# A convolution and mixer kernel: one idle product less ahead of the band, masks moved, and the low-rank sums of batch 0 regrouped

## The chip, the cores and the metric

One core of one Trainium2 chip. The metric is device time in microseconds (us) of one execution; most executions of one kernel agree within 0.3%.

## The reference

```python
# x: (8, 4224, 192); weight: (8 heads, 7 taps); U: (4224, 32); V: (32, 4224)
w = softmax(weight)                          # per head
y = causal 7-tap convolution of x, per head  # 24 channels per head
h = y.transpose(0, 2, 1) @ U @ V             # low rank, over the sequence
u = y + h.transpose(0, 2, 1)
out = u + relu(u @ w_ch1) @ w_ch2            # 192 -> 768 -> 192
```

## The kernel before

The convolution runs on TensorE as a product with a banded matrix ("band"), built at the start in two halves of four heads each. Batch 0 is the prologue: nothing can overlap it. Its x comes in four pieces, each of some blocks of 64 rows; the low-rank sums `y^T U` of its 33 tiles follow as pieces finish. The parts that matter (cuts marked `...`):

```python
    zz = cst.tile([P, 512], F32, name="zz")
    nc.vector.memzero(zz[:])

    rq = cst.tile([P, 2], F32, name="rq")
    for r in range(4):
        for n, v in enumerate((32.0, -128.0)):
            nc.vector.memset(rq[QB * r : QB * r + QB, n : n + 1], v * r)
    wps = bank()

    def idle(n):
        for _ in range(n):
            nc.tensor.matmul(out=wps[:], lhsT=zz[:, 0:P], rhs=zz[:], start=True, stop=True)

    idle(5)
...                                  # VectorE makes ident, and the products pr of both halves
    Eq = cst.tile([P, 4, P], BF16, name="Eq")
    nc.vector.tensor_scalar(
        out=Eq[:], in0=efp[:], scalar1=rq[:, 1:2], scalar2=None, op0=ALU.is_equal
    )

    nc.vector.tensor_scalar(
        out=fp[:], in0=fp[:], scalar1=R - 1, scalar2=None, op0=ALU.bitwise_and
    )
    R4 = cst.tile([P, P], BF16, name="R4")
    nc.vector.tensor_scalar(
        out=R4[:], in0=fp[:], scalar1=0.0, scalar2=None, op0=ALU.is_equal
    )

    def band_half(hh):
        bp = bank()
        for d in range(KC):
            nc.tensor.matmul(
                out=bp[:, 0 : HQ * BW],
                lhsT=ident[:],
                rhs=prs[hh][:, d, :, :],
                start=(d == 0),
                stop=(d == KC - 1),
            )
        for r in range(4):
            o = QB * (r % 2)
            evac(
                "AD"[hh],
                bands[hh][QB * r : QB * r + QB, :, o : o + BW],
                bp[QB * r : QB * r + QB, 0 : HQ * BW].rearrange("p (h t) -> p h t", h=HQ),
            )
...
    band_half(0)
    idle(1)
    band_half(1)
...
    def tt_split(b, p):

        hi = sml.tile([P, D], BF16, name="tt_hi")
        lo = sml.tile([P, D], BF16, name="tt_lo")
        nc.scalar.activation(out=hi[:], in_=p[:, 0:D], func=ACT.Copy)
        nc.vector.tensor_tensor(out=lo[:], in0=p[:, 0:D], in1=hi[:], op=ALU.subtract)
        ttb[b] += [hi, lo]

    def tt_done(b, p):
        t = sml.tile([P, D], BF16, name="tt_sb", bufs=3)
        nc.vector.tensor_copy(out=t[:], in_=p[:, 0:D])
        ttb[b] = t
...
    for h in range(0, H, 2):
        conv(0, h, 2, [0, 1], "AA" if h == 0 else "AD", *KP[0][1:])
    work = [bank() for _ in range(4)]
    u_layout(work)
    x_tile(1)
    x_zero(1, nc.gpsimd)
    x_part(1, *XP[0])
...
    ps0 = bank()
    parts0 = [(0, 0, 2, bank(), "A"), (0, 2, 4, bank(), "D"), (1, 0, 4, bank(), "D")]
    yT_part(0, parts0)
    conv_piece(2, work[0:3])
    tt_mm(0, piece_tiles(0) + piece_tiles(1), work[3])
    tt_split(0, work[3])
    conv_piece(3, work[0:3])
    tt_late(ps0, late[0], 0, True, False)
    for part in ttb[0]:
        nc.tensor.matmul(out=ps0[:, 0:D], lhsT=R4[:], rhs=part[:], start=False, stop=False)
    tt_late(ps0, late[1], len(late[0]), False, True)
    more = [(2, 0, 2, bank(), "A"), (2, 2, 4, bank(), "A")]
    yT_part(0, more)
    tt_done(0, ps0)
    hT_part(0, parts0 + more)
```

`idle` products are fp32, and each shows as two passes in the traces (five products, x10); they only warm the array. `evac` copies a PSUM bank to SBUF on ScalarE ("A") or VectorE ("D"). There are eight banks, used in rotation. A sum "on column tiles" (`tt_mm`) uses 32 of the array's 128 columns, four tiles at a time; a "full-width" sum (`tt_late`) uses weights repeated four times. `tt_split` writes a sum as two bf16 parts, tt_hi on ScalarE and then tt_lo on VectorE; the two R4 products add the four column groups up.

## Time and profile before

| | kernel before |
|---|---|
| median of all 6 runs beside the changed kernel | 326.88 us (326.1 to 327.98) |
| span of the profiled execution | 325.0 us |
| first low-rank product on TensorE | 18.68 us |
| end of the last TensorE product | 320.96 us |
| landing of the last store | 323.88 us |

All positions are in us from the start of the span of the profiled execution. The prologue ends with the first low-rank product; the four last rows divide the span into a prologue (18.7), the steady stretch (302.3), the landing of the last stores (2.9) and a closing barrier (1.1). Copies of a kernel's result from a PSUM bank to SBUF are called evacuations below; a number like L365 is a line of the kernel.

### The profile page before, as it was taken

The numbers are of one execution on the slowest core, as the hardware profiler recorded it, in microseconds if no ns is written. First come the engines' busy times: TensorE is split into PE (matmuls) and PEld (weight loads), VectorE is DVE, ScalarE is ACT, GpSimd is POOL, SyncE is SP. The second block draws the span as 40 slices with busy tenths as digits, with TensorE's granted clock in tenths as the row PEclk, the third lists the DMA queues.
The fourth block names the chain that finished last, engine by engine and source line by source line (L and its number), as shares of the span: only waits on it lengthen the run. The fifth ranks groups of instructions, "written<-read, shape, count | busy, mean of one in ns | idle before, by whom it ended". The sixth has DMA issues, their size and how long they took to land.

```text
span 325.0 us, 9590 instructions
## 1 busy us (share of the span) xinstructions
PE 318.6 (98%) x3998; PEld 223.9 (69%) x3998; DVE 269.5 (83%) x552; ACT 170.1 (52%) x343; POOL 143.6 (44%) x112
## 2 busy tenths in 40 slices
PE   8999999999999999999999999999999999999995
PEld 3766676478677747867864784587796497497494
DVE  7759999987987986998798699879888898896863
ACT  1667624860775397088339609824904903903910
POOL 8684179729946694786859497000000000000000
PEclk9999999999999999999999999999999999999999
DMA  9999993998996899599699957139168069048044
GB/s 106 193 183 180 200 217 102 193 200 252 199 156 177 234 171 169 168 188 180 159 235 150 221 150 195 47 110 240 49 183 255 3 159 280 2 120 269 2 135 159
DMA packets 122907, 53.52 MB, mean 165 GB/s; under 512 B 87760, under 2 KB 122832, under 8 KB 122864
## 3 DMA queue, kind: packets, MB, share of 16 engines
q1 hardware_dynamic: 84528, 38.08, 46.3%
q0 software_dynamic: 38192, 14.73, 39.4%
q8 instruction: 31, 0.51, 0.6%
q14 instruction: 12, 0.10, 0.1%
q10 hardware_dynamic: 144, 0.10, 0.1%
HBM read 29.49 MB, written 25.95 MB: 171 GB/s over the span
## 4 chain that ended last, share of the span: by engine, by line
PE 94%; DVE 4%; ACT 1%; issue 0%
PE ps L579 42%; PE ps L550 39%; PE ps L335 3%; PE ps L453 3%; PE ps L155 2%; PE ps L398 2%; DVE rl_sb L566 1%; PE ps L365 1%; ACT rl_sb L564 1%; DVE y_sb L254 1%; DVE u_sb L475 1%; PE ps L520 0%; PE ps L505 0%; DVE band L254 0%; PE ps L678 0%; PE ps L424 0%
## 5 line engine op out<-in xcount | busy, mean ns | idle before, releaser
L564 ACT ACTIVATE rl_sb<-ps 128x512 bf16<-128x512 f32 x233 | 124.3, 604 | 108.0 <-PE ps L550 96.0
L579 PE MATMUL ps<-W_sb,rl_sb 128*128 128x192 bf16 x1584 | 141.9, 246 | 0.1
L579 PEld LDWEIGHTS <-rl_sb 128*128 128x128 bf16 x1584 | 128.0, 98 | 13.5 <-issue 13.0
L550 PE MATMUL ps<-uT,W_sb 64*128 64x512 bf16 x1188 | 131.7, 376 | 0.0
L566 DVE TENSOR_SCALAR rl_sb<-ps 128x512 bf16<-128x512 f32 x163 | 105.3, 687 | 15.7 <-PE ps L550 15.4
L550 PEld LDWEIGHTS <-W_sb 64*128 64x128 bf16 x1188 | 66.7, 94 | 60.6 <-issue 3.8
L588 DVE TENSOR_TENSOR out_sb<-ps,u_sb 128x384 f32<-128x384 f32 (+1 forms) x133 | 70.3, 549 | 25.7 <-PE ps L579 24.4
L301 POOL COPY xb_sb<-x_sb 32x3072 bf16<-32x3072 bf16 (+1 forms) x24 | 67.6, 2826 | 0.7
L475 DVE TENSOR_TENSOR u_sb<-y_sb,ps 128x192 bf16<-128x192 bf16 (+1 forms) x168 | 66.2, 459 | 0.0
L289 POOL COPY xb_sb<-x_sb 128x3072 bf16<-128x3072 bf16 x12 | 32.6, 2744 | 34.4 <-PE ps L335 25.7
L252 ACT ACTIVATE y_sb<-ps 128x408 bf16<-128x408 f32 (+4 forms) x89 | 37.8, 512 | 10.4 <-PE ps L335 7.8
L79 POOL DMA_DIRECT2D x_sb<-in_x_dram x32 | 27.1, 851 | 17.7 <-PE ps L550 10.8
L254 DVE CAST y_sb<-ps 128x408 bf16<-128x408 f32 (+4 forms) x37 | 19.7, 577 | 0.8 <-PE ps L365 0.7
L453 PE MATMUL ps<-tt_sb,V_sb 32*128 32x192 bf16 x264 | 12.4, 246 | 0.2 <-DVE y_sb L254 0.2
L335 PE MATMUL ps<-x_sb,band 64*32 64x384 bf16 x192 | 12.1, 333 | 0.0
L335 PE MATMUL ps<-xb_sb,band 64*32 64x384 bf16 x192 | 12.1, 332 | 0.0
L453 PEld LDWEIGHTS <-V_sb 32*128 32x128 bf16 x264 | 4.7, 92 | 7.5 <-issue 7.5
L155 PE MATMUL ps<-zz 128*128 128x512 f32 x12 | 8.2, 836 | 1.5 <-DVE zz L145 1.5
L412 ACT ACTIVATE tt_hi<-ps 128x192 bf16<-128x192 f32 x8 | 2.7, 332 | 11.2 <-PE ps L398 11.2
L365 PE MATMUL ps<-x_sb,band 64*64 64x240 bf16 (+3 forms) x192 | 8.0, 276 | 0.4 <-DVE band L254 0.4
L365 PEld LDWEIGHTS <-band 64*64 64x64 bf16 x192 | 6.0, 106 | 2.2 <-issue 1.2
L335 PEld LDWEIGHTS <-band 64*32 64x32 bf16 x384 | 4.5, 89 | 4.1 <-issue 3.0
(65 smaller groups left out, 72.9 us busy)
## 6 DMA issues: line engine op xcount, KB each, us to landing
out_dram<-out_sb SPq DMA_DIRECT2D x131, 192.0 KB, 2.7
x_sb<-in_x_dram POOLq DMA_DIRECT2D x14, 384.0 KB, 7.6
x_sb<-in_x_dram POOLq DMA_DIRECT2D x7, 432.0 KB, 7.3
x_sb<-in_x_dram POOLq DMA_DIRECT2D x7, 408.0 KB, 7.5
x_sb<-in_x_dram POOLq DMA_DIRECT2D x1, 504.0 KB, 7.5
uT<-u_sb SPq DMA_TRANSPOSE x31, 4.2
x_sb<-in_x_dram POOLq DMA_DIRECT2D x1, 480.0 KB, 5.7
W_sb<-in_moe_w_ch_dram POOLq DMA_DIRECT2D x2, 192.0 KB, 8.0
```

What stands on the lines that cost most here:

```text
L79: return nc.gpsimd.dma_start(out=xt[b][HB * r : HB * r + HB, s0:s1, :], in_=x[b, blk * HB : (blk + s1 - s0) * HB, :].rearrange("(j p) d -> ...
L252: nc.scalar.activation(out=out, in_=in_, func=ACT.Copy)
L289: nc.gpsimd.tensor_copy(out=xbt[b][:, s0:s1, :], in_=xt[b][:, s0 + 1 : s1 + 1, :])
L301: nc.gpsimd.tensor_copy(out=xbt[b][q, s0:s1, :], in_=xt[b][q, s0:s1, :])
L335: nc.tensor.matmul(out=pp[r][QB * cg : QB * cg + QB, 0 : nk[r] * GS], lhsT=w[hr], rhs=t[hr, st : st + 2 * nk[r] - 1 : 2, hs], start=True, ...
L453: nc.tensor.matmul(out=banks[pr][:, a * D : (a + 1) * D], lhsT=V_sb[32 * q : 32 * q + 32, (j // 8) * 2 + j % 2, :], rhs=ttb[b][32 * q : 32 ...
L475: nc.vector.tensor_tensor(out=u_group(g)[:, i : i + n, :, hf, :], in0=yt[b][:, run[0] : run[0] + n, :].rearrange("p n (c k) -> p n c k", c=3),
L550: last = nc.tensor.matmul(out=pps[m][hf][:], lhsT=W1_sb[HB * hf : HB * hf + HB, c, m * P : (m + 1) * P], rhs=uTt[g][HB * hf : HB * hf + HB ...
L564: nc.scalar.activation(out=rl[:, m, hf, :], in_=pp[hf][:], func=ACT.Relu)
L566: nc.vector.tensor_scalar_max(out=rl[:, m, hf, :], in0=pp[hf][:], scalar1=0.0)
L579: last = nc.tensor.matmul(out=cps[:, a * D : (a + 1) * D], lhsT=rlt[g][:, m, hf, (i + a) * P : (i + a + 1) * P], rhs=W2_sb[:, m, :], start ...
L588: nc.vector.tensor_tensor(out=o[:, 0:n, :].rearrange("p n (c k) -> p n c k", c=3), in0=cps[:, 0 : n * D].rearrange("p (n c k) -> p n c k", ...
```

## The change

Intent: take one idle product (and the start-up of a wide zero tile) out from ahead of the band, let VectorE evacuate the band's second half before it makes two masks that are needed later, and do 27 instead of 20 sums of batch 0 on column tiles, which are cheaper on TensorE than full-width ones.

```diff
@@ x pieces
-    KP = [(0, 0, 10), (1, 0, 10), (1, 10, NB1 // 2), (0, 10, NB0 // 2)]
+    KP = [{0: (0, 10), 1: (0, 10)}, {1: (10, NB1 // 2)}, {0: (10, NB0 // 2)}]
 ... (x_piece, piece_tiles, conv follow the new form; the same four loads in the same order)
@@ idle products
-    zz = cst.tile([P, 512], F32, name="zz")
+    zz = cst.tile([P, P], F32, name="zz")
-            nc.tensor.matmul(out=wps[:], lhsT=zz[:, 0:P], rhs=zz[:], start=True, stop=True)
-    idle(5)
+            nc.tensor.matmul(
+                out=wps[:].rearrange("p (n t) -> p n t", t=P),
+                lhsT=zz[:],
+                rhs=zz[:].unsqueeze(1).to_broadcast([P, 4, P]),
+                start=True,
+                stop=True,
+            )
+    idle(4)
@@ masks: these two move from ahead of band_half to behind u_layout(work)
-    nc.vector.tensor_scalar(
-        out=fp[:], in0=fp[:], scalar1=R - 1, scalar2=None, op0=ALU.bitwise_and
-    )
-    R4 = cst.tile([P, P], BF16, name="R4")
-    nc.vector.tensor_scalar(
-        out=R4[:], in0=fp[:], scalar1=0.0, scalar2=None, op0=ALU.is_equal
-    )
@@ sums of batch 0
-    late = [piece_tiles(k) for k in (2, 3)]
+    late = piece_tiles(2)
 ... (U4_sb and its copy shrink to the 6 tiles of late)
     work = [bank() for _ in range(4)]
+    tp = bank()
-    conv_piece(2, work[0:3])
-    tt_mm(0, piece_tiles(0) + piece_tiles(1), work[3])
-    tt_split(0, work[3])
-    conv_piece(3, work[0:3])
-    tt_late(ps0, late[0], 0, True, False)
-    for part in ttb[0]:
-        nc.tensor.matmul(out=ps0[:, 0:D], lhsT=R4[:], rhs=part[:], start=False, stop=False)
-    tt_late(ps0, late[1], len(late[0]), False, True)
+    conv_piece(1)
+    tt_mm(0, piece_tiles(0), tp, last=False)
+    conv_piece(2)
+    tt_mm(0, piece_tiles(1), tp, len(piece_tiles(0)))
+    tt_split(0, tp)
+    ps0 = work[3]
     more = [(2, 0, 2, bank(), "A"), (2, 2, 4, bank(), "A")]
-    yT_part(0, more)
+    yT_part(0, more[0:1])
+    tt_late(ps0)
+    for n, part in enumerate(ttb[0]):
+        nc.tensor.matmul(out=ps0[:, 0:D], lhsT=R4[:], rhs=part[:], start=False, stop=(n == 1))
+    yT_part(0, more[1:])
     tt_done(0, ps0)
```

More of the change, by code (lines that the diff above doesn't have):

```diff
@@ L84 @@
     XP = [(0, 1, 17), (0, 17, NB0 + 1), (1, 0, 18), (1, 18, NB1 + 1)]
-    KP = [(0, 0, 10), (1, 0, 10), (1, 10, NB1 // 2), (0, 10, NB0 // 2)]
+    KP = [{0: (0, 10), 1: (0, 10)}, {1: (10, NB1 // 2)}, {0: (10, NB0 // 2)}]
     def x_piece(k):
-        r, k0, k1 = KP[k]
-        x_part(0, r, (1 - r if k0 == 0 else 2 * k0 + 1), 2 * k1 + 1)
+        for r, (k0, k1) in KP[k].items():
+            x_part(0, r, (1 - r if k0 == 0 else 2 * k0 + 1), 2 * k1 + 1)
     def piece_tiles(k):
-        r, k0, k1 = KP[k]
-        return [NB0 // 2 * r + j for j in range(k0, k1)]
+        return [NB0 // 2 * r + j for r, ks in KP[k].items() for j in range(*ks)]
     x_tile(0)
-    for k in range(2):
-        x_piece(k)
+    x_piece(0)
     I32 = mybir.dt.int32
@@ L129 @@
     nc.gpsimd.dma_start(out=Ur[0:nlast, nfull, :], in_=U4[nfull * P :, :])
-    for k in range(2, len(KP)):
+    for k in range(1, len(KP)):
         x_piece(k)
@@ L349, in conv32, with conv @@
                 )
-    def conv(b, h0, nh, rs, engs, k0=0, k1=NT, pp=None):
+    def conv(b, h0, nh, rs, engs, ks=((0, NB0 // 2), (0, NB1 // 2)), pp=None):
         if yt[b] is None:
             yt[b] = ys.tile([P, NT, D], BF16, name="y_sb")
-        nk = {r: min(k1, (NB0, NB1)[r] // 2) - k0 for r in rs}
+        nk = {r: ks[r][1] - ks[r][0] for r in rs}
         if pp is None:
@@ L363, in conv @@
                     for c in range(2):
-                        st = 1 - halo + c + 2 * k0
+                        st = 1 - halo + c + 2 * ks[r][0]
                         last = nc.tensor.matmul(
@@ L381, in conv @@
         for n, r in enumerate(rs):
-            j0 = NB0 // 2 * r + k0
+            j0 = NB0 // 2 * r + ks[r][0]
             evac(
@@ L390, with tt_mm @@
     ttb = [[] for _ in range(B)]
-    def tt_mm(b, js, p=None):
+    def tt_mm(b, js, p=None, o=0, last=True):
         if p is None:
             p = bank()
-        for n, j in enumerate(js):
+        end = o + len(js)
+        for n, j in enumerate(js, o):
             c = n % 4
@@ L402, in tt_mm @@
                 start=(n < 4),
-                stop=(n + 4 >= len(js)),
+                stop=last and n + 4 >= end,
                 tile_position=(0, 32 * c),
@@ L669, with tt_late @@
         LOADS[b] = [(g, 0), (g, 3), (g + 1, 0), (g + 1, 3)]
-    late = [piece_tiles(k) for k in (2, 3)]
-    U4_sb = cst.tile([P, sum(len(js) for js in late), 4, R], BF16, name="U4_sb")
-    def tt_late(p, js, o, first, last):
-        for n, j in enumerate(js):
+    late = piece_tiles(2)
+    U4_sb = cst.tile([P, len(late), 4, R], BF16, name="U4_sb")
+    def tt_late(p):
+        for n, j in enumerate(late):
             nc.tensor.matmul(
                 out=p[:, 0:D],
-                lhsT=U4_sb[:, o + n, :, :].rearrange("p a r -> p (a r)"),
+                lhsT=U4_sb[:, n, :, :].rearrange("p a r -> p (a r)"),
                 rhs=yt[0][:, j, :],
-                start=first and n == 0,
-                stop=last and n + 1 == len(js),
-            )
-    def conv_piece(k, pps):
-        r, k0, k1 = KP[k]
-        for n, h in enumerate(range(0, H, 3)):
-            conv(0, h, min(3, H - h), [r], "AD"[n % 2], k0, k1, {r: pps[n]})
+                start=(n == 0),
+                stop=False,
+            )
     for h in range(0, H, 2):
-        conv(0, h, 2, [0, 1], "AA" if h == 0 else "AD", *KP[0][1:])
+        conv(0, h, 2, [0, 1], "AA" if h == 0 else "AD", KP[0])
     work = [bank() for _ in range(4)]
+    tp = bank()
     u_layout(work)
+    nc.vector.tensor_scalar(
+        out=fp[:], in0=fp[:], scalar1=R - 1, scalar2=None, op0=ALU.bitwise_and
+    )
+    R4 = cst.tile([P, P], BF16, name="R4")
+    nc.vector.tensor_scalar(
+        out=R4[:], in0=fp[:], scalar1=0.0, scalar2=None, op0=ALU.is_equal
+    )
     x_tile(1)
@@ L698 @@
     o = 0
-    for js in late:
+    for r, (k0, k1) in KP[2].items():
+        j = NB0 // 2 * r + k0
         nc.gpsimd.tensor_copy(
-            out=U4_sb[:, o : o + len(js), :, :],
+            out=U4_sb[:, o : o + k1 - k0, :, :],
             in_=U_sb[:]
-            .rearrange("p k j r -> p (k j) r")[:, js[0] : js[-1] + 1, :]
+            .rearrange("p k j r -> p (k j) r")[:, j : j + k1 - k0, :]
             .unsqueeze(2)
-            .to_broadcast([P, len(js), 4, R]),
+            .to_broadcast([P, k1 - k0, 4, R]),
         )
-        o += len(js)
+        o += k1 - k0
     NSL = (NT + 7) // 8 * 2
@@ L725, with conv_piece @@
     nc.gpsimd.dma_start(out=W2_sb[:], in_=moe_w_ch2[:].rearrange("(m p) d -> p m d", p=P))
-    ps0 = bank()
     parts0 = [(0, 0, 2, bank(), "A"), (0, 2, 4, bank(), "D"), (1, 0, 4, bank(), "D")]
     yT_part(0, parts0)
-    conv_piece(2, work[0:3])
-    tt_mm(0, piece_tiles(0) + piece_tiles(1), work[3])
-    tt_split(0, work[3])
-    conv_piece(3, work[0:3])
-    tt_late(ps0, late[0], 0, True, False)
-    for part in ttb[0]:
-        nc.tensor.matmul(out=ps0[:, 0:D], lhsT=R4[:], rhs=part[:], start=False, stop=False)
-    tt_late(ps0, late[1], len(late[0]), False, True)
-    more = [(2, 0, 2, bank(), "A"), (2, 2, 4, bank(), "A")]
-    yT_part(0, more)
+    def conv_piece(k):
+        for n, h in enumerate(range(0, H, 3)):
+            for r in KP[k]:
+                conv(0, h, min(3, H - h), [r], "AD"[n % 2], KP[k], {r: work[n]})
+    conv_piece(1)
[4 more added lines that the diff above has]
+    ps0 = work[3]
+    more = [(2, 0, 2, bank(), "A"), (2, 2, 4, bank(), "A")]
+    yT_part(0, more[0:1])
[3 more added lines that the diff above has]
+    yT_part(0, more[1:])
     tt_done(0, ps0)
```

## The prediction

> **What bounds the kernel now.** I read the busy table first, then the stretches of the span, then the chain of waits over the first 22 us, which is all that the change touches.
>
> ```profile
> PE 318.6 (98%) x3998; PEld 223.9 (69%) x3998; DVE 269.5 (83%) x552; ACT 170.1 (52%) x343; POOL 143.6 (44%) x112
> ```
>
> ```profile
> 21.00:38.00 17.00, 16.94 (x181) 10.41 (x180) 15.32 (x29) 11.54 (x24) 7.41 (x15) 1.00 1.49 181
> 38.00:160.00 122.00, 121.66 (x1647) 86.61 (x1644) 104.72 (x217) 70.91 (x148) 87.00 (x50) 1.00 1.07 188
> ```
>
> TensorE (first busy figure) has no holes from 21 us on: 16.94 of 17.00, 121.66 of 122.00. So the kernel is a prologue of 21 us and then 300 us of a full TensorE that the change leaves alone. Whatever the prologue gains, the end gains, once and no more: 1% of the span is 3.3 us, and the whole prologue is 21.
>
> The prologue's chain:
>
> ```profile
> 1.47 7.11 PE ps L155 x10
> 8.57 0.46 PE ps L232 x7
> 9.04 0.90 PE ps L155 x2
> 9.94 0.47 PE ps L232 x7
> ...
> 11.42 0.33 DVE band L254
> 11.75 0.04 issue
> 11.80 1.01 PE ps L365 x30
> 12.80 0.59 PE ps L260 x15
> 13.40 0.57 PE ps L505 x16
> 13.96 1.28 PE ps L365 x32
> 15.24 0.53 PE ps L398 x20
> 15.77 1.12 PE ps L365 x32
> 16.89 0.69 PE ps L678 x7
> 17.57 0.17 PE ps L736 x2
> 17.73 0.51 PE ps L678 x6
> 18.24 0.02 issue
> 18.27 0.37 DVE tt_sb L418
> ```
>
> L155 are the idle products (they warm the array and compute nothing), L232 builds the band, L365 is the convolution, L260 lays out U, L505 transposes y, L398 sums 20 tiles on column tiles, L678 sums 13 tiles with full-width weights. The reader should see that idle products stand directly ahead of both halves of the band, and that the convolution waits for VectorE's evacuation of half two.
>
> **What the Trainium skill says.** "TensorE: Matmul & The Clock Gate", Part 1, says that the array starts at half rate and reaches full rate after a busy window of some 3.4 us, and that this window is free-running. The trace agrees: idle passes start every 0.854 us until 6.69 us and every 0.429 us after. So the length of the idle stretch depends on where that switch falls in a run. "TensorEngine Tiling (Array Packing)", Tiling Modes, says that tiles work independently, up to four for 32 columns, and that a change of mode drains the array. The trace agrees: 20 column-tiled sums took 0.53 us of the chain (27 ns each), 13 full-width ones 0.69 + 0.51 = 1.20 us (92 ns each). The same page, PSUM Bottleneck, warns that tiling does not speed up evacuation, which is the warning that matters here. The skill has nothing that settles when the x pieces land; that I take from the trace.
>
> **The change part by part.**
>
> *Idle products.* Each is two passes. The zero tile shrinks from 512 to 128 columns; its memset took 0.48 us for 512 columns and a 256-column one 0.27, so about 0.17 us for 128: TensorE starts 0.31 earlier, at 1.16. One product less removes two late passes, 0.86 us at full rate. Eight passes from 1.16, six or seven of them slow, end near 7.38 instead of 8.41. VectorE's two products pr run 6.05 to 8.49, 1.26 each, so the first is ready at 7.3, just in time: half one of the band starts about 1.03 us earlier. The single idle product between the halves stays (0.90), so half two starts at 8.75 (its pr is ready at 8.49), also 1.03 earlier.
>
> *The masks.* fp and R4 (0.27 + 0.23 us on VectorE) move behind the U layout. Half two leaves TensorE at 9.4. VectorE was then free before as well (R4 ended at 9.34, the evacuation began at 10.44), so without the move the two would just have met; the move itself is worth 0 to 0.1 us. Evacuation ends at 10.72 instead of 11.75.
>
> *The x pieces.* They are issued in the same order and at the same times. The second one is the catch:
>
> ```profile
> 2.28 0.94 POOL L79 DMA_DIRECT2D x_sb<-in_x_dram  x1
> ...
> x_sb<-in_x_dram POOLq DMA_DIRECT2D x1, 504.0 KB, 7.5
> ```
>
> 2.28 + 7.5 = 9.8 us. The convolution started at 10.33, held by ScalarE's evacuation of half one (9.07 + 1.20 = 10.27). That now ends at 9.24, but the third product of the convolution reads the second piece, so it starts at about 9.85: of 1.03 us only 0.48 are left. The old stall for band half two goes, apart from under 0.1 us, so TensorE would end the convolution about 1.1 us earlier.
>
> *ScalarE then takes over.* It evacuates five of the eight convolution results, one every 0.47 us:
>
> ```profile
> 10.97 2.42 ACT L252 ACTIVATE y_sb<-ps 128x480 bf16<-128x480 f32 x5 [0.70 <-PE ps L365]
> 13.43 0.69 ACT L252 ACTIVATE U_sb<-ps 128x288 bf16<-128x288 f32 x2
> ```
>
> It began 0.64 us after the convolution did, so now at 10.49, and its queue is only 0.48 earlier. The buffers rotate through eight banks. The U layout's third product needs the bank freed by the third evacuation (10.49 + 1.49 = 11.98), the transposes' second part that of the fifth (12.91), and the next convolution piece the first U evacuation (about 13.37). TensorE arrives ahead of each and waits. So the second convolution piece starts at about 13.44 instead of 13.89: gain 0.45. Its x piece landed at 5.72 + 7.3 = 13.0, the next at 6.50 + 8.0 = 14.5, needed at 15.2; both hold.
>
> *The sums.* Order is now: piece (1.28), 20 sums (0.52), piece (1.12), 7 sums on column tiles, split, 6 full-width sums, two R4 products. Seven sums of 92 ns become seven of about 27: about 0.45 us less TensorE work. But the split now follows the last piece. Before, it lay under that piece (ScalarE at 15.82, VectorE at 16.18). Now ScalarE first finishes its last evacuation (17.34 before, so 16.90), then tt_hi (0.33) to 17.27, then VectorE tt_lo (0.36) to 17.66, and the second R4 product starts at 17.70. TensorE has only six sums to do meanwhile (16.95 to 17.45). The old path ran last evacuation 17.34, last sum started at 17.98: 0.64. The new one runs 16.90 to 17.70: 0.80. The regrouping thus loses some 0.16 us although it takes work off TensorE. tt_sb is ready at 18.34 instead of 18.63.
>
> Sum: +0.45 up to the second piece, -0.16 in the tail, 0.28 to 0.3 us gained at the first low-rank product. GpSimd's copy of U for the full-width sums shrinks from 13 tiles to 6 (0.93 us less), off the path: its loads are paced by landings.
>
> **The rivals.** *The whole of the idle time comes through:* 1.0 us, plus 0.4 from cheaper sums, so about 325.9. For it: L155 is on the chain, L678 too. Against: the landing at 9.8 and the evacuation queue. *The warm-up falls otherwise:* if the clock switches 1.5 us later, the old convolution starts near 11.1, the new one still near 9.9, and the gain is about 1 us; if it switches earlier, both wait for x and the tail's 0.16 us is lost: 327.4. *The tail costs more:* if the R4 products wait longer for the split, or TensorE's wait before the convolution dropped the clock, nothing is gained or 0.5 us lost: 327.5 to 328. The wait is about 0.6 us, short beside the 5 us that the start-up took, so I doubt the second.
>
> **Range and chances.** The runs of before spread from 326.25 to 327.57, mean 327.06. Less 0.28, with a little weight on the later switch, that is 326.8. The run-to-run spread of 0.7 either way and the rivals from 325.9 to 327.5 give 325.7 to 327.9. A gain over 2% needs 6.5 us, a third of the prologue; nothing here can give that. Faster 0.01, within 2% 0.98, slower 0.01.
>
> **What would show it right or wrong.** In the changed profile: idle products ending near 7.4; band half one at 7.4; the first convolution at 9.8 to 9.9, released by the landing and no longer by an evacuation; no stall of 0.36 for band half two; new short waits of TensorE on ScalarE in the U layout and the transposes; a wait on VectorE tt_lo before the last R4 product; tt_sb ending at about 18.3. I am wrong if the convolution starts before 9.7 (then x was not the limit), if the convolution pieces follow with no wait for ScalarE, if no wait on tt_lo appears, or if an idle gap over 0.2 us opens after 21 us, which would mean that the early gain is given back.

## The result, and the profile after

The changed kernel took 325.56 us in the median of 6 runs (325.4 to 325.79), the kernel before 326.88. The ratio is 0.9958 (95% interval 0.9935 to 0.998). Ratios here are the mean time of one kernel's fast runs over that of the other's of the same rounds, so not quite the ratio of the medians quoted. The gain is 1.4 us by the means (326.94 and 325.56), under 2% as foretold, but 325.56 lies below the stated range, which began at 325.7. The predicted gain of 0.28 us was five times too small.

The two profiled executions divide it:

| | before | after | difference |
|---|---|---|---|
| second convolution piece starts | 13.89 | 13.11 | -0.78 |
| first low-rank product | 18.68 | 18.09 | -0.59 |
| last TensorE product ends | 320.96 | 320.38 | -0.58 |
| last store lands | 323.88 | 322.47 | -1.41 |
| span | 325.0 | 323.8 | -1.2 |

So two things differ from the prediction: the prologue gained 0.59 in this pair, and 0.83 more was gained after TensorE had finished (1.41 - 0.58), where nothing had been looked at. (The closing barrier gave 0.2 of it back.) The steady stretch passes the prologue's gain on, to 0.01 us.

The chain of waits of the changed kernel, in the prologue:

```profile
2.28 7.42 DMA x_sb<-in_x_dram
9.70 0.04 issue
9.75 2.01 PE ps L361 x62
...
13.18 1.28 PE ps L361 x32
...
14.98 1.12 PE ps L361 x32
16.10 0.28 PE ps L395 x7
...
16.65 0.66 PE ps L675 x6
17.30 0.08 PE ps L746
17.39 0.01 issue
17.40 0.26 PE ps L746
```

Idle products and band have left the chain: it now begins with the load of the second x piece, which lands at 9.70, and the convolution follows 0.05 later. That is what the prediction had said. The last lines show the regrouped sums: seven on column tiles (L395), six full-width (L675), the two R4 products (L746).

The end of the two traces, the DMA view from the end of TensorE's work on (queue: packets, MB, share of the engines' time; then stores: KB each, us from issue to landing). Before:

```profile
q14 instruction: 1, 0.01, 1.1%
...
out_dram<-out_sb SPq DMA_DIRECT2D x1, 192.0 KB, 2.8
out_dram<-out_sb SPq DMA_DIRECT2D x1, 96.0 KB, 2.6
out_dram<-out_sb ACTq DMA_DIRECT2D x1, 96.0 KB, 2.5
```

After:

```profile
out_dram<-out_sb SPq DMA_DIRECT2D x1, 192.0 KB, 1.9
out_dram<-out_sb SPq DMA_DIRECT2D x1, 96.0 KB, 1.8
out_dram<-out_sb ACTq DMA_DIRECT2D x1, 96.0 KB, 1.7
```

Before, one 8 KB fetch of instructions (it starts at 321.67) lies among the last three stores, and these need 2.5 to 2.8 us; after, no fetch lies there, and they need 1.7 to 1.9. The fetch itself took 0.71 us, and at the end of these stores, from 322.6 us on, the last bytes came at some 22 GB/s for 0.8 us, after 320 to 420 GB/s up to there (the GB/s line of the same view); the view after has no such tail. That these bytes had stood behind the fetch is an inference. In the changed kernel VectorE's program is two instructions shorter (two separate waits became unnecessary when the order changed), and the fetch in question starts at 324.29, after everything has landed. That gave theory F: the fetch is one of VectorE's program, and its place depends on how many instructions VectorE has.

### The profile page after: what moved, and what is told of

Its sections match the earlier page's. It is cut to its first block, busy times and chain, and to the rows that moved or that the text cites. A ratio compares the mean times of both kernels' runs of the same rounds, so it can differ in the third digit from the quotient of the medians.

```text
span 323.8 us, 9582 instructions
## 1 busy us (share of the span) xinstructions
PE 318.3 (98%) x3996; PEld 223.4 (69%) x3996; DVE 269.6 (83%) x552; ACT 169.9 (52%) x343; POOL 142.6 (44%) x111
## 4 chain that ended last, share of the span: by engine, by line
PE 92%; DVE 3%; DMA 2%; ACT 1%; issue 0%; POOL 0%; POOLq 0%
PE ps L576 42%; PE ps L547 39%; PE ps L331 3%; PE ps L450 3%; DMA x_sb<-in_x_dram 2%; PE ps L395 2%; PE ps L361 1%; DVE rl_sb L563 1%; ACT rl_sb L561 1%; DVE y_sb L250 1%; DVE u_sb L472 1%; PE ps L502 1%; PE ps L517 0%; PE ps L421 0%; POOL x_sb L79 0%
## 5 line engine op out<-in xcount | busy, mean ns | idle before, releaser
L153 PE MATMUL ps<-zz 128*128 128x512 f32 x10 | 7.2, 875 | 1.1 <-DVE zz L143 1.1
```

## The experiments

Sixteen runs were made, four of them repeats of a kernel without an edit; all were correct.

### Is the end's gain the instruction fetch, or chance? (runs 1, 2, 7)

Run 1, the kernel before with four VectorE instructions fewer, where VectorE is idle:

```diff
-        for n, v in enumerate((32.0, -128.0)):
-            nc.vector.memset(rq[QB * r : QB * r + QB, n : n + 1], v * r)
+        nc.vector.memset(rq[QB * r : QB * r + QB, 0:1], 32.0 * r)
+    nc.vector.tensor_scalar(
+        out=rq[:, 1:2], in0=rq[:, 0:1], scalar1=-4.0, scalar2=None, op0=ALU.mult
+    )
```

> The kernel before with four instructions fewer in VectorE's stream (a constant tile is made from 4 memsets and a multiply, in a stretch where VectorE is idle), nothing else. Theory F (the last 8 KB instruction fetch, at 321.7 us of the profile before, falls among the last stores and delays their landing; the changed kernel has two VectorE instructions fewer and escapes it): the first low-rank product stays at 18.7 us, the fetch moves behind the landing of the last stores, these land in 1.7 us instead of 2.5 to 2.6, span 0.5 to 0.9 us shorter (about 324.2), times about 326.1, and the kernel before's second group of times near 327.5 is gone. Theory C (landing times of the last stores vary by chance, or with the time at which the kernel ends): times as the kernel before in the same rounds, 326.1 to 328.0 in two groups.

Measured: 325.80 us median (325.31 to 326.42) against 326.73 for the kernel before in the same rounds, ratio 0.997 (0.9957 to 0.9982). The fetch moved to 324.06, the last store landed in 1.67 us. The first low-rank product came at 18.09, not 18.7: the array's clock had risen early in that execution (see below).

Run 2, the changed kernel with two memsets added, so that VectorE's program is as long as before:

```diff
+    for n in range(2):
+        nc.vector.memset(rq[0:QB, n % 2 : n % 2 + 1], 0.0)
```

> The changed kernel with two idle memsets added to VectorE's stream early on, so that its length is that of the kernel before. Theory F: the prologue stays (first low-rank product at 18.1 us), but the instruction fetch is back among the last stores, which land in 2.5 us or more; about 0.6 to 1 us slower than the changed kernel, 326.2 to 327. Theory C: 325.6 as the changed kernel, last stores landing in 1.7 us.

Measured: 326.51 us median (326.38 to 326.81), ratio to before 0.9992. The same view of its end:

```profile
q14 instruction: 1, 0.01, 1.1%
...
out_dram<-out_sb SPq DMA_DIRECT2D x1, 96.0 KB, 2.9
out_dram<-out_sb ACTq DMA_DIRECT2D x1, 96.0 KB, 2.8
```

Two idle memsets at the start of the kernel bring the fetch back to 321.02 and the last stores back to 2.8 us and more, 320 us later. Theory F holds in both directions; by the means the fetch is worth 0.95 us (326.78 - 325.83 in run 1's rounds).

Run 7, the kernel before once more (no edit):

> The kernel before once more, for its profile. Theory F: an 8 KB instruction fetch between 321 and 322.5 us and last stores landing in 2.4 us or more. On the array's clock: the first low-rank product follows the end of the five idle products, so it comes at 18.7 us if the slow passes end at 6.7 us as in the first profile, near 18.1 if they end before 5.5, near 19.1 if they end at 8.

Measured: 326.97 us; a fetch at 321.47, last stores landing in 2.9 to 3.2 us, first low-rank product at 18.45. All three traces with that program length (before, runs 2 and 7) have the fetch among the stores; in the 15 others the last store landed in 1.66 or 1.67 us. Theory C, chance, is out. The traces also show that the place of the fetch follows the length of VectorE's program: with 707 VectorE records it starts 0.71 to 0.73 us after the last TensorE product, with 706 (runs 3, 4, 9, 12 and 14) 1.66 to 1.84, with 702 to 705 (the other ten) 3.66 to 3.93. With 706 it still starts 0.25 to 0.43 us before the last landing and delays nothing, so it matters when the fetch comes, and not only whether it lies among the stores.

### What the front is worth, and what the sums are worth (runs 3, 4, 6, 9)

Run 3 has the change's front (idle products, zero tile, masks) with the x pieces and sums of before; run 4 is the reverse.

```diff
 run 3: kernel before
-    idle(5)
+    idle(4)          # with the small zero tile; masks behind u_layout(work)
 run 4: changed kernel
-    idle(4)
+    idle(5)          # with the 512-column zero tile; masks ahead of band_half
```

> The kernel before with the front of the change (one idle product less, small zero tile, masks moved), but its own x pieces and sums: 20 sums on column tiles with their split under the next piece, 13 full-width sums. Theory S (the regrouped sums lose 0.2 us because the split is exposed behind the last piece): second convolution piece at 13.1 us, first low-rank product at 17.9 us, 0.2 us earlier than the changed kernel. Theory W (fewer TensorE passes over the sums are worth 0.45 us): first low-rank product at about 18.5 us. Time under S, if the fetch stays clear of the stores: about 325.4, else near 326.

> The changed kernel with the front of the kernel before put back (five idle products, the 512-column zero tile, masks early); only the x pieces' grouping and the sums differ from before. Theory S: second convolution piece at 13.9 us as before, first low-rank product at 18.9 us, 0.2 us later than before; time 0.2 us over the kernel before less whatever the place of the last fetch gives. Theory W: first low-rank product at 18.2 us.

Measured: run 3 325.15 us (325.05 to 325.68), ratio 0.9952; run 4 326.16 us, ratio 0.9977. From the second convolution piece to the first low-rank product run 3 takes 4.79 us, as before, and run 4 4.94; the changed kernel takes 4.98. So the regrouped sums lose, as theory S had it, and the front gains: 325.27 against 325.83 of run 1 by the means of the same rounds, neither delayed by the fetch, is 0.56. (By the same means the regrouped sums alone, run 4 at 326.17, cost 0.33, and 0.56 - 0.33 = 0.23 is also what run 2 gained on the kernel before, 326.78 - 326.55, with the fetch among the stores in both.) The positions themselves missed (18.42 and 19.28 instead of 17.9 and 18.9), because in both executions the clock rose late and in run 3 x landed late, at 10.22. Its timeline shows how strictly the convolution follows that landing:

```profile
10.27 0.57 PE L363 MATMUL ps<-x_sb,band 64*64 64x240 bf16 x13 [0.45 <-DMA x_sb<-in_x_dram]
```

Run 6 is run 3 with run 1's four VectorE instructions fewer; run 9 is run 3 again, beside the changed kernel. Runs 5 and 10 are the changed kernel in the same rounds as 6 and 9 (no edit).

> The front of the change with the sums of the kernel before, and four VectorE instructions fewer, so that the last fetch is well clear of the stores. Theory S: second convolution piece to first low-rank product 4.79 us, 0.2 to 0.4 us faster than the changed kernel of the same rounds: 325.0 to 325.3. Theory W: slower than the changed kernel by 0.3 to 0.4 us.

> The front of the change with the sums of the kernel before (as the third run), now in the same rounds as the changed kernel. Theory S: second convolution piece to first low-rank product 4.79 us, and 0.2 to 0.4 us faster than the changed kernel: 325.1 to 325.4 against 325.5 to 325.7. Theory W: slower than the changed kernel.

> The changed kernel once more, as the yardstick of this chip for the next run. Theory F with S: 325.4 to 325.8; last fetch behind the landing of the last stores, these land in 1.7 us; second convolution piece to first low-rank product 4.98 us.

> The changed kernel in the same rounds: 325.5 to 325.7, 4.98 us from the second convolution piece to the first low-rank product, last fetch behind the landing of the last stores.

Measured: run 6 325.36 against 325.62 us of run 5, run 9 325.31 against 325.62 of run 10 (medians of the same rounds; a single execution of 327.29 in run 6 and one of 328.7 in run 10 are outliers, treated below). Run 6 missed its 325.0 to 325.3 by a little. With the sums of before it is 4.79 and 4.83 us from piece to product, with the regrouped ones 4.92 and 5.28. So the front with the old sums is the fastest version that ran, by about 0.3 us; that is 0.1% and only the medians and the traces carry it, as the outliers blur the means.

### What bounds the front (runs 8, 11, 12)

```diff
 run 8:  KP = [{0: (0, 9), 1: (0, 10)}, {1: (10, NB1 // 2)}, {0: (9, NB0 // 2)}]
 run 11: between the halves of the band
-    idle(1)
+    idle(0)
 run 12: the two masks back ahead of band_half
```

> The changed kernel with one block of 64 rows fewer in the first x piece of row half 0 (9 instead of 10; the last piece takes it). Theory L (in the changed kernel the convolution waits for the landing of the second x piece): the two pieces carry 1.92 MB instead of 2.02, the second lands 0.27 us earlier, at 9.4 us, and the convolution's third product starts 0.05 us after the landing. Theory B (it waits for the band): it starts where it does in the changed kernel, at 9.7 us. The first low-rank product moves by less than 0.2 us in either, as the last piece and its sums grow.

> The changed kernel without the idle product between the two halves of the band (0.9 us of TensorE time less, straight on the way to band half two). Theory L (the second x piece bounds the front): the convolution's third product still starts 0.05 us after that piece lands, near 9.7 us; half two is there earlier, which takes at most the 0.1 us of waiting ahead of the fifth head away; first low-rank product at 17.9 to 18.1 us, as in the changed kernel. Theory B (TensorE's own work ahead of the band bounds it): first low-rank product at 17.2 us.

> The changed kernel with the two VectorE masks back in front of the evacuation of band half two. They end near 9.4 us, when that half leaves TensorE, so the evacuation starts at most 0.05 us later (9.43 instead of 9.38); first low-rank product within 0.1 us of 18.1. If the move of the masks carried part of the gain, it would come 0.4 us later or more.

Measured: in run 8 (325.66 us) the second piece landed at 9.59, not 9.4, so the edit hardly moved what it was to move; the third product followed 0.04 later. By itself that run decides little. In run 11 the idle product vanished from ahead of half two and the third product still came 0.04 us after the landing, at 9.57; first low-rank product at 17.75, not 17.2. By itself this run is weaker than its expectation says, since half two came only 0.18 us earlier (8.54 for 8.72): TensorE waited for VectorE's second product there. What decides is all traces together: in the 14 with the new front and in run 1 the third product starts 0.04 us after the landing, and these landings lie anywhere from 9.53 to 10.22; in the other three (before, runs 4 and 7) the band is later than the landing, and the third product starts 0.35 to 1.02 us after it. The front of the changed kernel is bound by the landing, theory L. (Run 11's time, 329.11, has another cause, below.) Run 12 (325.43 us): half two's evacuation starts at 9.38, as in the changed kernel. In this trace moving the masks is worth nothing.

### Why the regrouped sums lose (runs 10, 13 to 16)

The loss had been predicted, with a cause: the split is exposed. Run 10 spoke against that. Its timeline:

```profile
16.96 0.36 DVE L410 TENSOR_TENSOR tt_lo<-ps,tt_hi 128x192 bf16<-128x192 f32 x1 [0.31 <-ACT tt_hi L409]
...
17.29 0.25 PE L746 MATMUL ps<-tt_hi,R 128*128 128x192 bf16 x1
17.85 0.24 PE L746 MATMUL ps<-tt_lo,R 128*128 128x192 bf16 x1 [0.32 <-issue]
```

tt_lo is done at 17.32, and the product that needs it could follow the one before by 0.08 us, at 17.37. It starts at 17.85, and the releaser is "issue": TensorE waited for nothing that the profile shows. In the changed kernel it is the same with 17.17 and 17.40. In all six traces with these sums and this TensorE program (the changed kernel and runs 2, 5, 10, 12 and 16) the late product starts 2.25 to 2.31 us after the start of a 16 KB instruction fetch on another queue (15.11 and 17.40 in the changed kernel, 15.59 and 17.85 in run 10). The changed kernel's, in the DMA view from 15.09 to 15.14 us:

```profile
q8 instruction: 1, 0.02, 118.2%
```

Theory P: TensorE has used up its instructions at this point and waits for the next ones. The four next runs shift TensorE's program and leave the sums alone:

```diff
 run 13: changed kernel, four TensorE instructions fewer
-    idle(4)
+    idle(3)
 runs 14 (kernel of run 3) and 15 (changed kernel): two idle products as two halves each, eight more
+            if halves > 0:
+                for q in range(2):
+                    nc.tensor.matmul(out=wps[:, 2 * P * q : 2 * P * q + 2 * P] ..., [P, 2, P] ...)
 run 16: the changed kernel (no edit)
```

> The changed kernel with three idle products ahead of the band instead of four: four TensorE instructions fewer, in a stretch whose end is set by VectorE's products and the x landing. Theory P (TensorE runs out of instructions at the second R4 product and waits for a fetch): that point moves four instructions on, past the R4 products, to transposes that precede a wait anyway; second R4 product 0.08 us after the first, second convolution piece to first low-rank product 4.80 us instead of 4.98, times 0.1 to 0.2 us below the changed kernel. Theory S (the exposed split): 4.98 us and the same times.

> The kernel with the change's front and the sums of before (4.79 us from the second convolution piece to the first low-rank product in all six traces with those sums), with two idle products cut in two halves each: eight TensorE instructions more, no more work. Theory P: the point at which TensorE runs out comes forward into the second group of full-width sums; one of them, or the product after it, starts 0.1 us or more late, 2.3 us after a fetch began, and the 4.79 us become 4.85 to 5.1. Theory S: 4.79 us.

> The changed kernel with the same eight instructions more. Theory P: TensorE runs out at the fourth of the six full-width sums, which then starts 2.3 us after the fetch began; what follows it is pushed back, 5.0 to 5.2 us from the second piece to the first low-rank product. The second R4 product follows the first by 0.08 us. Theory S: 4.98 us, and the second R4 product late as before.

> The changed kernel in the same rounds: 325.5 to 325.7, 4.93 to 5.0 us from the second piece to the first low-rank product (more where the fetch comes late), second R4 product 2.26 to 2.31 us after the fetch began.

| | piece to product, us | what starts late | after the fetch began |
|---|---|---|---|
| changed kernel | 4.98 | second R4 product, 0.18 | 2.29 |
| run 13 (-4) | 4.81 | nothing on the path | - |
| run 3 / run 14 (+8) | 4.79 / 4.99 | nothing / last full-width sum, 0.22 | - / 2.29 |
| run 15 (+8) | 5.31 | fourth of six sums, 0.50 | 2.26 |
| run 16 (0) | 5.25 | second R4 product, 0.45 | 2.31 |

Run 13's timeline, for comparison with run 10's:

```profile
16.84 0.36 DVE L410 TENSOR_TENSOR tt_lo<-ps,tt_hi 128x192 bf16<-128x192 f32 x1 [0.31 <-ACT tt_hi L409]
...
17.17 0.25 PE L746 MATMUL ps<-tt_hi,R 128*128 128x192 bf16 x1
17.25 0.25 PE L746 MATMUL ps<-tt_lo,R 128*128 128x192 bf16 x1
```

tt_lo ends at 17.20 and its product starts at 17.25, in its own slot. And run 15's sums, with the stall moved in among them:

```profile
16.61 0.41 PE L686 MATMUL ps<-y_sb,U_sb 128*128 128x192 bf16 x3
17.36 0.41 PE L686 MATMUL ps<-y_sb,U_sb 128*128 128x192 bf16 x3 [0.34 <-issue]
```

The late product is whichever stands at the same place in TensorE's program: counted from the first idle pass it is TensorE's 223rd matmul in each of the nine traces with a late product on the path (the six above, runs 14 and 15, and run 4, whose one idle product more brings the stall into the last of the six sums, 0.14 us). Run 11, which also has four TensorE instructions fewer, takes 4.81 us like run 13. And eight instructions that do no extra work brought the stall into the old sums too. Theory P stands and theory S is wrong about the cause: with the split where the change puts it, but the fetch out of the way, the regrouped sums take 4.81 us, equal to the old ones. (Run 15 missed its 5.0 to 5.2: the stall came at the fourth sum, as expected, but cost 0.50 us.) Run 14's time was 325.45 us, run 15's 325.87, run 16's 325.81 in the median, a little over its 325.5 to 325.7. (The expectation of run 14 gives 4.79 us for six traces; run 9's is 4.83. Run 8, with seven full-width sums, takes 5.13.)

Run 13's times missed their expectation: 326.99 us in the median, 325.61 to 328.0, although its prologue did what theory P said. Its trace loses 0.8 us between 79 and 85 us. That, and the outliers of other runs, is the next point.

### Outliers, in all kernels

Run 16's profiled execution took 330.0 us, and shows what such runs are. First the waits between 70 and 90 us, then the stretches (length; busy time of PE, PEld, DVE, ACT, POOL; granted clock; DMA share; GB/s):

```profile
DVE out_sb L585 <- DMA out_dram<-out_sb: 3.3, 1, 3.3
```

```profile
80.00:82.00 2.00, 0.75 (x7) 0.44 (x6) 0.98 (x3) 0.00 (x0) 1.44 (x1) 1.00 1.10 368
84.00:86.00 2.00, 2.00 (x14) 1.10 (x13) 2.00 (x5) 0.00 (x0) 2.00 (x1) 0.50 0.85 165
```

Stores issued at 71 to 73 us took 9.4 us to land (6.5 in the changed kernel's first trace); loads of x and a DMA transpose were under way beside them (the transpose took 12.3 us to land, 7.9 in the first trace), and what slowed them stays open. The eight output buffers were then all in flight, VectorE waited 3.3 us for one, TensorE fell idle for 1.2 us, and from 83.07 us on it was granted half its clock for 3.4 us. Run 11's trace has the same pair of events, which is its 329.11: VectorE starts at 80.13, 0.13 us after a store that took 9.4 us landed (the view puts this wait down to a TensorE product that ended at 80.09, but the twelve that this output needs ended at 77.65), TensorE is idle for 0.65 us, and the clock is halved from 82.58 to 85.99. Run 13's trace has the first event alone: a store of 7.6 us, and VectorE waits 1.2 us. Executions of 327.29 (run 6), 328.7 (changed kernel) and 329.16 (kernel before, 1 of 11 in those rounds) have no trace; that they are the same is an inference. Why four of six executions of run 13 are slow, and whether a prologue that ends at a certain time invites this, stays open.

## Why the prediction was wrong, point by point

- **"Whatever the prologue gains, the end gains, once and no more."** This step failed. The steady stretch passed the gain on exactly, but the end had a gain of its own of 0.83 us in the profiled pair and 0.95 by the means of run 1: an 8 KB fetch of VectorE's program that lay among the last stores, and that the change moved away by making VectorE's program two instructions shorter. I had not looked behind the last product. The page of the kernel before shows the fetches (12 on that queue, 11 after). My own table of stretches had the hint, in its last row, which the prediction left out: TensorE busy for 160.94 of 165.00 us, the rest being the end. So what failed is the step from the prologue to the whole time; the next points take the prologue apart.

```profile
160.00:325.00 165.00, 160.94 (x1908) 115.02 (x1906) 135.62 (x267) 78.22 (x152) 33.13 (x18) 1.00 0.60 146
```

- **The net of the prologue, 0.28 us.** Right on average: the changed kernel at 325.56 to 325.64 against 325.83 of run 1, which has only the fetch taken away, is 0.2 to 0.3, and run 2 against the kernel before 0.23. The profiled pair gave 0.59, a trace of either kernel being one draw. That the net came out right is partly luck: by the means the front gave more than predicted (0.56 for 0.45) and the sums lost more (0.33 for 0.16), the latter for another cause.
- **The range.** Its sums don't follow from its base: the rival that lets all the idle time come through is 327.06 - 1.4 = 325.66, not 325.9, and the loss of the tail alone is 327.06 + 0.16 = 327.2, not 327.4. The base was also the mean of the first three executions; all six give 326.94.
- **Front: +0.45.** The bound was named rightly, the second x piece, and is shown by the 15 traces in which the convolution follows its landing. The size was 0.78 in the pair. The mis-sized term is ScalarE's start: I carried over 0.64 us from the convolution's start to the first evacuation; it was 0.54 (9.75 to 10.29), since the two products that do not need the second piece had run already. ScalarE's pace was also better, 0.45 us an evacuation instead of 0.47, and x landed 0.06 earlier.
- **ScalarE takes over.** Right by the trace: the third product of the U layout starts at 11.84, 0.05 after the third evacuation ended, and the transposes' second part at 12.77, 0.05 after the fifth. No run tested it apart.
- **The masks: 0 to 0.1.** Right; run 12's trace says 0.
- **Sums: -0.16.** The size was right in the pair (0.19; 0.13 to 0.49 over the traces), and this is luck, for the cause was wrong: not the exposed split but TensorE waiting for its own instructions. The split was just hidden: in run 13 it ends at 17.20 and its product starts in its own slot at 17.25. One of the prediction's signs of being wrong did come true, as no wait on tt_lo appears in the changed kernel's trace. A term was mis-sized too: the seven sums on column tiles took 0.28 us of the chain, 40 ns each and not 27.
- **The rival on the clock.** It is real, and it belongs to the kernel before. With five idle products the end of these followed the rise of the clock. The idle products of run 1 and of run 4, whose front is the old one:

```profile
1.47 6.15 PE L157 MATMUL ps<-zz 128*128 128x512 f32 x10 [1.47 <-DVE zz L145]
```

```profile
1.47 7.55 PE L153 MATMUL ps<-zz 128*128 128x512 f32 x10 [1.47 <-DVE zz L143]
```

They end at 7.62 and 9.02 us, at 8.57 in the first trace of before, and the second convolution piece follows, at 13.30, 14.34 and 13.89. With the new front the idle products ended anywhere from 6.2 to 7.8 and the third product of the convolution always began 0.04 to 0.05 after the landing. This fits the smaller spread of the changed kernel (0.39 us over its first six executions, 1.9 before); run 1, with the old front and without the delayed stores, spreads by 1.1.

## What to carry to other kernels

When a change moves the end by more than the path it touches, look past the last compute instruction: stores at the very end have nothing to hide behind, and an instruction fetch among them cost 0.95 us here, more than the whole intended change gained. A change to the number of VectorE's or TensorE's instructions moved the later fetches of that engine here; so before a gain of a few tenths is put down to a mechanism, shift the program by a few idle instructions and see whether it stays. And "issue" as the releaser of an idle stretch, in a dense run of short matmuls, is a reason to look for a fetch, here 2.3 us earlier.

## What the Trainium skill lacked or had wrong

- "Trainium Architecture — The Big Picture", The software stack, says that the instruction streams are brought into each engine's instruction memory when the program is loaded. "Runtime: NRT & Kernel Launch", Instruction fetch mechanics, has the rest: blocks of 16 KiB (256 instructions) are fetched while the program runs, at a cost that is "mostly hidden". The runs agree on the blocks of one queue (31 in the execution, 0.51 MB; by that page an estimate of 7,936 instructions, close to the 7,996 matmuls and weight loads that the page of the kernel before counts on TensorE), but the other queue's are of 8 KB. And the runs show two places where the cost was not hidden, which no page has: a fetch delayed stores (0.95 us) and starved TensorE (0.12 to 0.50 us, the product starting 2.25 to 2.31 us after the fetch in nine traces). That the second queue's fetch is VectorE's is inferred from the program lengths above; that the first's are TensorE's, from runs 13 to 15 and the count of 223.
- "TensorE: Matmul & The Clock Gate", Part 1, has the free-running window of some 3.4 us. The runs agree: full clock came between 4.0 and 7.5 us of the span in 18 traces, and after an idle spell the clock was halved for 3.4 us, in an execution some 4 us longer with the waits around it. It puts the whole ramp at under 1% of a typical span, and that fits: with the old front, half one of the band started between 7.46 and 8.85 us in four traces, a spread of 0.4% of the span. What it lacks is a warning that such a spread, with warm-up products on the path, exceeds a gain like the 0.28 us looked for here.
- "TensorEngine Tiling (Array Packing)", PSUM Bottleneck, warns of the evacuation. Here sums that were to be 0.45 us cheaper brought nothing (4.81 against 4.79 us): in run 13 the six sums that remain wait for ScalarE's last evacuation (it ends at 16.58, they start at 16.68), and TensorE fills the time before them with four transposes (0.23 us of the chain). Nothing in the page is wrong.
